# The first two batches of a packed-attention and two-layer MoE kernel, reordered by a list scheduler in single-engine steps

## The chip, the cores and the metric

The kernel runs on one core of one Trainium2 chip. The metric is the device time of one execution in microseconds (us), the median of several runs. The engines are TensorE (PE; its weight loads are PEld), VectorE (DVE), ScalarE (ACT), GpSimd (POOL) and SyncE (SP), which issues every DMA here.

## The reference

Eight batches, eight heads, 576 tokens, head dimension 64, 32 packed rows for each head, all in fp32. Attention runs twice: the packed rows `p` attend to `k`, `v`, and their result serves `q` as both keys and values. Two dense layers follow.

```python
def sm_attn(qq, kk, vv):
    s = scale * np.matmul(qq, kk.transpose(0, 1, 3, 2))
    s = s - np.max(s, axis=-1, keepdims=True)
    a = np.exp(s)
    a = a / (np.sum(a, axis=-1, keepdims=True) + 1e-09)
    return np.matmul(a, vv)
p_packed = sm_attn(p, k, v)
out = sm_attn(q, p_packed, p_packed)
x = out.transpose(0, 2, 1, 3).reshape(4608, 512)
h = np.maximum(np.maximum(x @ w1, x @ w2), x @ w3)   # w1..w3: 512 x 768
x = h @ w_out                                        # 768 x 512
h = x @ w_in                                         # 512 x 2048
return (h * np.cos(h)) @ moe2_w_out                  # 2048 x 512
```

## The kernel before, in words

A number that needs more than TensorE's fp32r format is kept as two halves, high (rounded) and low (the rest), and a product is three matmuls over the halves (`passes`). `split` makes them: a copy on ACT, a subtraction on DVE or POOL.

**Units.** A batch has two units (groups of four heads). Phase 1 of a unit makes its packed values: `ld_k`, `ld_v` (loads), `S1` (scores, 8 native fp32 matmuls), `S1m` (maximum), `E1` (exponential), `v` (halves of the values), `T1` (transposes), `PV1` (packed values), `BT` (their transpose, in two layouts `bt` and `wt`). Phase 2 makes the attention of the queries: `ld_q`, `S2` (scores), `S2t`, `S2r` (transpose to 32-wide blocks, maximum, subtraction), `X2a` (exponential), `X2b` (sum, reciprocal, multiplication), `X2t` (transpose back), `X2c` (halves). Batch 0 uses `Unit32`, whose `PV1` multiplies the raw values in native fp32 and needs no `v`; the others use `Unit`.

**Folds.** The packed values are multiplied into w1, w2, w3 once for two batches: `fold(b, j, g, pi)` is a quarter of a column group `j` (five groups: four of 512 columns, one of 256). Its three matmuls write the PSUM tile `zps`, ACT and DVE split it into `zx`, of which there are two buffers in the first two batches, and SP sends one half of it to the tile `z` of the even batch and the other to DRAM (`zd`), where the odd batch fetches it (`load_z`). `fold_first(g)` makes a whole half of group 0 for batch 0 alone, in six matmuls straight into `z`.

**Dense layers.** `gemm1(b, u, m)`, u from 0 to 17, multiplies `z` by the attention (12 matmuls of 288 columns) and every third result ends a maximum over three. `gemm2` is the second product (36 such matmuls for each of four d). The last layers run after all batches, with tiles of 512 tokens.

**Weight pieces.** w1, w2, w3 and w_out arrive as 24 pieces of 512 KB, as 64-bit floats, and are rebuilt on the chip: `sign` (POOL), `wc` (ACT), two bit operations on DVE (`wc`, `wm`), a rounding copy (ACT) and `low` (POOL). `conv_wa` does one piece and also finishes the one before. Pieces 8 and on land in the pool `wop`, which is opened when both units of batch 0 are done.

**Order.** Each engine executes its instructions in program order. Before, this order is written by hand: `START` lists the steps ahead of the batches, `FIRST`, `PLAN`, `PLAN0` and `FOLDS` put steps at positions u of the batches, and each position of batch 0 also converts a piece. A step such as `T1` issues its instructions on PE, ACT and DVE at once.

Of the kernel before, what the change touches and what calls it, by code (L numbers as in the profile page):

```python
# [19 lines left out]
MAGIC = 12582912.0  # L20


@with_exitstack
def tile_pack_attention_max_moe_cos_moe(
# [98 lines left out]
    with tc.manual_schedule():  # L123
# [4 lines left out]
        class Res:  # L128
            def __init__(self):
                ap = self.ap = actx.enter_context(tc.tile_pool(name="ap", bufs=1, side="right"))  # L130
                self.ps = actx.enter_context(tc.tile_pool(name="ps_a", bufs=1, space=PSUM, side="right"))
                self.pz = ap.tile([P, 2, P], F32, name="pz")
                self.bt = [[ap.tile([P, 2, P], F32, name=f"bt{o}{g}") for g in range(NG)] for o in range(2)]
                self.wt = [wtp.tile([P, 8, D], F32R, tag="x", name="wt") for _ in range(NWT)]
                self.mask = ap.tile([P, P], F32, name="mask")
                self.vhl = ap.tile([P, 2, NCH, 2 * P], F32R, name="vhl")

            def clear(self):
                nc.gpsimd.memset(self.pz, 0.0)
# [10 lines left out]
        class Res32:  # L150
            def __init__(self, n, ps):
# [4 lines left out]
                if n == 0:  # L156
                    self.pz1 = self.ap.tile([P, 2, P], F32, name="pz1")
                    nc.vector.memset(self.pz1, 0.0)
# [32 lines left out]
        class Unit:  # L191
            def lo(self, name):
                return nc.gpsimd if name == "v" else nc.vector

            def __init__(self, b, g):
                self.b, self.g = b, g
                self.res = res32[g] if b == 0 else res
                self.pz = res32[g].pz if b == 0 else res32[0].pz1 if (b, g) == (1, 1) else res.pz
                self.bt = res.bt[b % 2][g]
                self.wt = res.wt[b // 2 % 2 * NG + g]  # L200
# [40 lines left out]

            def v(self):
                self.vhl = self.res.vhl
                for c, n, rows, r in self.vr:
                    src = r[:rows, :n * 2 * P].rearrange("p (a e) -> p a e", a=n)
                    split(self.vhl[:rows, 0, c:c + n, :], self.vhl[:rows, 1, c:c + n, :], src, self.lo("v"))
# [26 lines left out]
            def E1(self):  # L273
                self.e = self.etile()
                nc.gpsimd.memset(self.e[:, S:], 0.0)
                nc.scalar.activation(
# [13 lines left out]

            def T1(self):
                src = self.tr()[:, :SP_].rearrange("p (c b d) -> p c b d", b=2, d=D)
                self.at = self.res.ap.tile([P, 2 * SP_], F32R, tag="at", name="at")
                av = self.at.rearrange("p (c b d) -> p c b d", b=4, d=D)
                split(av[:, :, ::3, :], av[:, :, 1:3, :], src)

            def PV1(self):
                ps = self.big()
# [9 lines left out]
                pv = self.res.ap.tile([P, P], F32, tag="pv", name="pv")  # L308
                for pi in range(2):
                    own, oth = slice(pi * D, pi * D + D), slice(D - pi * D, P - pi * D)  # L310
                    nc.scalar.copy(pv[own], ps[oth, pi, :P])
                    for j in (1, 0):
                        nc.vector.tensor_tensor(  # L313
                            out=pv[own], in0=pv[own], in1=ps[own, pi, j * P:(j + 1) * P], op=ALU.add
                        )
                self.recip()
                self.bd = self.res.ap.tile([P, P], F32, tag="bd", name="bd")
                nc.vector.scalar_tensor_tensor(
                    out=self.bd, in0=pv, scalar=self.st[:, 3:4], in1=self.res.mask, op0=ALU.mult, op1=ALU.mult
                )  # L320
# [37 lines left out]
            def X2b(self):  # L358
                t = self.t
                tb = t[:, :S].rearrange("p (a b) -> p a b", b=32)  # L360
                sm = self.ms[:, 1, :]
                nc.vector.tensor_reduce(out=sm, in_=tb, op=ALU.add, axis=AX.X)
                nc.vector.tensor_scalar(out=sm, in0=sm, scalar1=EPS, scalar2=None, op0=ALU.add)
                nc.vector.reciprocal(out=sm, in_=sm)
                self.lo("mul").tensor_tensor(
                    out=tb, in0=tb, in1=sm[:, :, None].to_broadcast([P, NB, 32]), op=ALU.mult
                )

# [3 lines left out]

            def X2c(self):
                h = at[self.b, self.g] = hp.tile([P, 2, S], F32R, tag="h", name="at")
                split(h[:, 0, :], h[:, 1, :], self.a[:, :S], self.lo("X"))

        class Unit32(Unit):
            def T1(self):
                ps = self.tr()
                self.at = self.res.ap.tile([P, SP_], F32, tag="at", name="at")  # L380
                h = 3 * P
                nc.scalar.copy(self.at[:, :h], ps[:, :h])
                nc.vector.tensor_copy(self.at[:, h:], ps[:, h:SP_])

            def PV1(self):
                ps = self.big()[:, 0, :]
# [11 lines left out]
                self.recip()  # L398
                self.bd = self.res.ap.tile([P, P], F32, tag="bd", name="bd")
                for pi in range(2):  # L400
                    own = slice(pi * D, pi * D + D)
                    nc.vector.scalar_tensor_tensor(
                        out=self.bd[own], in0=ps[own, pi * P:(pi + 1) * P], scalar=self.st[own, 3:4],
# [11 lines left out]
        def fold(b, j, g, pi):  # L415
# [11 lines left out]
            nx[0] += b > 0  # L427
            x = (wop if nx[0] % 3 == 2 else zx).tile([P, 2, UB * P], F32R, tag="w", name="zx")[:, :, :nw]
            split(x[:, 0, :], x[:, 1, :], ps)
            if pi == 0 and (b, j) != (0, 0):  # L430
                zt[b, j, g] = zp.tile([P, 2, UB * P], F32R, tag="w", name="z")
            zo = zd[b + 1, j, g]
            own, oth = slice(pi * D, pi * D + D), slice(D - pi * D, P - pi * D)
            if (b, j) != (0, 0):
                z = zt[b, j, g][:, :, :nw]
                nc.sync.dma_start(out=z[own].bitcast(F32), in_=x[own].bitcast(F32))
            nc.sync.dma_start(out=zo[oth], in_=x[oth].bitcast(F32))

        def fold_first(g):
            wt = units[0][g].wt  # L440
            ps = fps[0].tile([P, 512], F32, tag="f", name="zps")
            n = 0
            for pi in range(2):
                for x, y in passes:
# [3 lines left out]
                        w_mov(0, 2 * g + pi, y),  # L448
# [4 lines left out]
            z = zt[0, 0, g] = zp.tile([P, 2, UB * P], F32R, tag="w", name="z")  # L453
            split(z[:, 0, :], z[:, 1, :], ps)

        def load_z(b, j):
            nw = min(UB, NU - j * UB) * P
            for g in range(NG):
                zt[b, j, g] = zp.tile([P, 2, UB * P], F32R, tag="w", name="z")
                nc.sync.dma_start(out=zt[b, j, g][:, :, :nw].bitcast(F32), in_=zd[b, j, g])  # L460

        def gemm1(b, u, m):
            j, c = u // UB, (u % UB) * P
            ps = ps_m.tile([P, 2, 512], F32, tag="big", name="h")
            for hf in range(2):
                n = 0
                for g in range(NG):
                    for x, y in passes:
# [7 lines left out]
                        n += 1  # L476
            if u % 3 == 0:
# [4 lines left out]
        def gemm2(b, d, hf, hh):  # L482
            if hf == 0:
                g2ps[0] = ps_m.tile([P, 2, 512], F32, tag="big", name="x2")
            ps = g2ps[0]
            n = 0
            for f in range(NF):
                w = wa[NU + f]
                for x, y in passes:
# [7 lines left out]
                    n += 1  # L497
            if hf:
                s = mp.tile([P, S], F32, tag="m", name="x2s")
                nc.vector.tensor_copy(halves(s), ps[:, :, :HS])  # L500
                o = 0
                while o < S:
                    t, r = divmod(b * S + o, TT)
                    k = min(S - o, TT - r)
                    nc.sync.dma_start(out=x2d[t][:, d, r:r + k], in_=s[:, o:o + k])
                    o += k

        g2ps = [None]
# [22 lines left out]
        PLAN = {  # L531
# [5 lines left out]
        }  # L537
        PLAN0 = {
# [343 lines left out]
```

## Time and profile before

| | |
|---|---|
| median of 3 runs | 1458.03 us (1452.14 to 1458.88) |
| the profiled execution | 1458.1 us, span of its instructions 1456.2 us |
| busy, share of the span | PE 95%, PEld 81%, DVE 58%, ACT 37%, POOL 19% |
| granted TensorE clock, mean | 0.973 of full speed |

The page also cuts the span into 40 equal slices, of 36.4 us each. There the digits of PE are 7, 5, 6, 6, 8 and then 9 nearly throughout, and the granted clock is 9, 6, 7, 7 and then 9: what is not filled lies in the first five slices. Times below count from the start of the span.

### The profile page before, as it was taken

To read this page: it belongs to the slowest core of one execution; us is meant where nothing else is said; L and a number is where in the kernel's file an instruction comes from. 1 tells how busy PE (TensorE), PEld (TensorE's weight loads), DVE (VectorE), ACT (ScalarE), POOL (GpSimd) and SP (SyncE) were. 2 spreads that over 40 slices of the span, in tenths; PEclk is the share of its full clock that TensorE was granted. 3 is DMA by queue.
4 is the path that set the end of the run, shared out by engine and by line. 5 is a ranking of instruction groups with operands and counts; after the bars stand their busy time and mean duration, and the time that the engine had idled before them with its cause. 6 is when DMAs were issued, how large, how long until landed. Compare 5 with 4: busy or idle time off the path is not lost.

```text
span 1456.2 us, 18953 instructions
## 1 busy us (share of the span) xinstructions
PE 1378.1 (95%) x7110; PEld 1180.3 (81%) x7110; DVE 847.7 (58%) x1423; ACT 535.4 (37%) x962; POOL 270.3 (19%) x229
## 2 busy tenths in 40 slices
PE   7566899999999999899999999999999999999998
PEld 4455899999989999788678888888888888888887
DVE  5655645555555556568875555555555555556554
ACT  3444232523342333444443333333333333333333
POOL 3765330303121213764500000000000000000000
PEclk9677999999999999899999999999999999999999
DMA  8285355843765478543210010100101010010000
GB/s 298 104 236 168 121 180 163 229 142 122 217 177 186 126 194 277 193 147 100 82 59 1 0 58 1 58 0 12 47 1 58 1 54 5 0 58 1 30 1 29
DMA packets 72860, 143.33 MB, mean 98 GB/s; under 512 B 13632, under 2 KB 35136, under 8 KB 72768
## 3 DMA queue, kind: packets, MB, share of 16 engines
q1 hardware_dynamic: 72768, 142.12, 31.6%
q8 instruction: 56, 0.92, 0.3%
q14 instruction: 36, 0.29, 0.1%
HBM read 86.51 MB, written 37.75 MB: 85 GB/s over the span
## 4 chain that ended last, share of the span: by engine, by line
PE 78%; DVE 12%; issue 3%; ACT 3%; DMA 2%; POOL 1%; SPq 0%; DVEq 0%; ACTq 0%; POOLq 0%
PE po L810 24%; PE g L709 24%; PE h L469 11%; PE x L490 9%; PE big L252 4%; PE zps L420 3%; PE big L301 1%; DMA zd<-zx 1%; DVE wm L110 1%; DVE m L480 1%; DVE wc L110 1%; DVE pv L313 1%; DVE wm L113 1%; DVE y L721 1%; DVE y L730 1%
## 5 line engine op out<-in xcount | busy, mean ns | idle before, releaser
L810 PE MATMUL po<-w,gh 128*128 128x512 f32 x1728 | 425.1, 395 | 3.9 <-ACT gh L74 3.3
L709 PE MATMUL g<-x,w 128*128 128x512 f32 x1728 | 419.1, 391 | 0.8 <-DVE x2s L500 0.8
L810 PEld LDWEIGHTS po<-w,gh 128*128 128x128 f32 x1728 | 324.0, 188 | 82.2 <-ACT gh L74 5.9
L709 PEld LDWEIGHTS g<-x,w 128*128 128x128 f32 x1728 | 324.3, 188 | 72.6 <-DVE x2s L500 1.1
L469 PE MATMUL h<-at,z 128*128 128x288 f32 x1728 | 263.6, 309 | 10.7 <-DVE x2s L500 3.7
L469 PEld LDWEIGHTS h<-at,z 128*128 128x128 f32 x1728 | 247.7, 197 | 19.1 <-DVE m L480 7.2
L725 ACT ACTIVATE y<-y 128x512 f32<-128x512 f32 x144 | 91.0, 632 | 245.2 <-DVE y L722 245.2
L490 PE MATMUL x<-hh,w 128*128 128x288 f32 x1152 | 163.4, 299 | 3.1 <-DVE hh L75 1.9
L490 PEld LDWEIGHTS x<-hh,w 128*128 128x128 f32 x1152 | 157.6, 190 | 8.1 <-DVE hh L75 3.6
L75 DVE TENSOR_TENSOR gh<-y,gh 128x512 fp32r<-128x512 f32 x144 | 99.8, 693 | 98.9 <-ACT gh L74 98.9
L730 DVE TENSOR_TENSOR y<-y,g 128x512 f32<-128x512 f32 x144 | 98.9, 687 | 92.7 <-ACT y L725 92.7
L74 ACT CAST gh<-y 128x512 fp32r<-128x512 f32 x144 | 89.4, 621 | 125.4 <-DVE y L730 124.3
L718 ACT ACTIVATE y<-g 128x512 f32<-128x512 f32 x144 | 86.2, 599 | 130.7 <-PE g L709 130.7
L720 DVE TENSOR_SCALAR y<-y 128x512 f32<-128x512 f32 x144 | 61.4, 426 | 115.8 <-ACT y L718 115.8
L721 DVE TENSOR_TENSOR y<-y 128x512 f32<-128x512 f32 x144 | 100.9, 701 | 6.1 <-DVE y L720 0.5
L480 DVE TENSOR_TENSOR m<-m,h 128x576 f32<-128x576 f32 x96 | 72.3, 753 | 43.6 <-PE h L469 32.2
L92 POOL TENSOR_SCALAR w<-wraw 128x512 fp32r<-128x512 f32 x56 | 90.8, 1623 | 17.7 <-DMA wraw<-w 12.0
L85 POOL TENSOR_TENSOR w<-wm,w 128x512 fp32r<-128x512 f32 x56 | 73.4, 1311 | 104.2 <-ACT w L106 78.7
L420 PE MATMUL zps<-w,wt 128*128 128x512 f32 (+1 forms) x240 | 67.0, 396 | 27.0 <-DVE zx L75 27.0
L75 DVE TENSOR_TENSOR zx<-zps,zx 128x512 fp32r<-128x512 f32 (+1 forms) x80 | 50.6, 635 | 71.9 <-ACT zx L74 63.3
L75 POOL TENSOR_TENSOR hh<-m,hh 128x576 fp32r<-128x576 f32 x40 | 56.9, 1423 | 169.0 <-ACT hh L74 168.8
L74 ACT CAST zx<-zps 128x512 fp32r<-128x512 f32 (+1 forms) x80 | 43.1, 541 | 94.0 <-PE zps L420 34.5
(87 smaller groups left out, 950.6 us busy)
## 6 DMA issues: line engine op xcount, KB each, us to landing
zd<-zx SPq DMA_DIRECT2D x64, 256.0 KB, 3.6
z<-zd SPq DMA_DIRECT2D x32, 512.0 KB, 4.5
z<-zx SPq DMA_DIRECT2D x60, 256.0 KB, 3.2
wraw<-w_out SPq DMA_DIRECT2D x22, 512.0 KB, 4.0
raw<-kT SPq DMA_DIRECT2D x32, 288.0 KB, 4.3
wraw<-w SPq DMA_DIRECT2D x18, 512.0 KB, 6.1
raw<-qT SPq DMA_DIRECT2D x32, 288.0 KB, 4.5
xr<-x2d SPq DMA_DIRECT2D x36, 256.0 KB, 5.1
```

What stands on the lines that cost most here:

```text
L74: nc.scalar.copy(hi, src)
L75: eng.tensor_tensor(out=lo, in0=src, in1=hi.bitcast(F32), op=ALU.subtract)
L92: nc.gpsimd.tensor_scalar(out=w[:, 1, :], in0=hi32.bitcast(F32), scalar1=0.0, scalar2=None, op0=ALU.mult)
L420: nc.tensor.matmul(ps, wt[:, pi * 4 + x * 2:pi * 4 + x * 2 + 2, :].rearrange("p a b -> p (a b)"), w_mov(j, 2 * g + pi, y), start=(n == 0), ...
L469: nc.tensor.matmul(ps[:, hf, :HS], zt[b, j, g][:, x, c:c + P], at[b, g][:, y, hf * HS:(hf + 1) * HS], start=(n == 0), stop=(n == 3 * NG - 1),)
L480: nc.vector.tensor_tensor(out=halves(m), in0=halves(m), in1=ps[:, :, :HS], op=ALU.max)
L490: nc.tensor.matmul(ps[:, hf, :HS], w[:, x, d * P:(d + 1) * P], hh[f][:, y, hf * HS:(hf + 1) * HS], start=(n == 0), stop=(n == 3 * NF - 1),)
L709: nc.tensor.matmul(ps, w[:, a, kc * P:(kc + 1) * P], x2[t, kc][:, b, :], start=(n == 0), stop=(n == 3 * KC - 1),)
L721: nc.vector.tensor_tensor(out=y, in0=y, in1=r, op=ALU.subtract)
L725: nc.scalar.activation(out=r, in_=y, func=AF.Sin, scale=TWO_PI)
L730: nc.vector.tensor_tensor(out=r, in0=r, in1=ps, op=ALU.mult)
L810: nc.tensor.matmul(po[t][s], g[:, a, s * P:(s + 1) * P], w[:, b, :], start=(f == 0 and i == 0), stop=(f == NF2 - 1 and i == 2),)
```

## The change

The steps are cut so that each issues on one engine (`T1` becomes `Tp`, `Ta`, `Td`; `fold` becomes `fold_p`, `fold_a`, `fold_d`, `fold_z`; a piece becomes `sg`, `wt`, `ws`, `wm`, `wh`, `wl`). For batches 0 and 1 and what belongs to batches 2 and 3 in that time, a class `Order` keeps a table of the steps with their assumed durations, needs and buffers, and issues them in the order in which it expects them to start; of those ready at nearly the same time it takes the one with the longest rest. `low` and the low half of `hh` go to POOL or DVE, and the copies out of `gemm2` to ACT or DVE, whichever is expected to end first. From batch 2 on the hand-written positions stay.

Batch 1 now also uses `Unit32`. Column groups 0 and 1 (`alone`) get folds of batch 0's own, `full_p`, `full_a`, `full_d`, in the manner of `fold_first`; their four quarters then serve batch 1 alone. The raw loads and the piece loads run as two sequences that the scheduler interleaves.

```diff
+class Order:
+    LAT, LAND, RATE, NEAR, BIAS = 0.2, 1.8, 0.34, 0.3, 0.4
...
+            for name, c in best.items():
+                near = min(x[0] for x in c) + self.NEAR
+                x = min((x for x in c if x[0] <= near), key=lambda x: (x[1], x[0]))
+                if pick is None or x[0] < pick[1][0]:
+                    pick = name, x
...
-        units = {b: [(Unit if b else Unit32)(b, g) for g in range(NG)] for b in range(B)}
+        units = {b: [(Unit if b > 1 else Unit32)(b, g) for g in range(NG)] for b in range(B)}
...
+        alone = (0, 1)
...
+            only = b == 0 and j in alone
...
+            if not only:
                 z = zt[b, j, g][:, :, :nw]
                 nc.sync.dma_start(out=z[own].bitcast(F32), in_=x[own].bitcast(F32))
...
-        def fold_first(g):
+        def full_p(j, g):
             wt = units[0][g].wt
-            ps = fps[0].tile([P, 512], F32, tag="f", name="zps")
+            nw = min(UB, NU - j * UB) * P
+            ps = fx[j, g] = fps[0].tile([P, 512], F32, tag="f", name="zps")[:, :nw]
...
+        LOADS = "k0 k1 v0 v1 q0 q1 k2 k3 v2 v3 q2 q3 k4 v4 k5 v5 k6 v6 q4 k7 v7 q5 k8 v8".split()
...
+            add(
+                ("W", n), "SP", 0.6, lambda n=n: load_wa(n), ["wop"] * (n >= 8),
+                [(pool, ("W", n))], data=0.52,
+            )
...
+            add(
+                ("wl", n), (GE, VE), (1.28, 0.7), lambda eng, n=n: low(wa[n], wm[n], EITHER[eng]), [("wh", n)], [],
+                [("wm", n)],
+            )
...
+                add(
+                    last, "PE", 1.6, lambda b=b, u=u: gemm1_p(b, u), after, [("mm", ("h", b, u))],
+                    [("Z", b, j, g) for g in range(NG)] + [("att", 2 * b + g) for g in range(NG)],
+                )
...
+        order.run()
...
-        for b in range(B):
+        for b in range(2, B):
```

What this does to the order is seen best at three places.

PE, around the first `gemm1`. Before (`zps<-w,wt` from L445 is `fold_first`, `raw,pz` is `S1`, `ident,e` the transposes, `vhl,at` `PV1`, `ident,bd` `BT`, and `h<-at,z` from L469 `gemm1`):

```order
L445 MATMUL zps<-w,wt 128x512 x6
L252 MATMUL big<-raw_199,pz_160 128x288 x4
L288 MATMUL big<-ident,e 128x128 x5
L301 MATMUL big<-vhl,at 128x256 x10
L288 MATMUL big<-ident,e 128x128 x5
L469 MATMUL h<-at,z 128x288 x12
L329 MATMUL big<-ident,bd 128x128
L301 MATMUL big<-vhl,at 128x256 x10
```

Now (L648 is `full_p`, L573 the fp32 `PV1` of batch 1, L685 `gemm1`):

```order
L648 MATMUL zps<-w,wt 128x512 x6
L407 MATMUL big<-ident,e 128x128 x5
L685 MATMUL h<-at,z 128x288 x12
L367 MATMUL big<-raw_199,pz_139 128x288 x4
L685 MATMUL h<-at,z 128x288 x24
L573 MATMUL big<-raw_200,at 128x256 x4
L573 MATMUL big<-raw_201,at 128x256
L648 MATMUL zps<-w,wt 128x512 x6
```

Three steps of `gemm1` now stand ahead of batch 1's `PV1`, and unit 3's scores stand behind the first of them.

DVE, in phase 2 of batch 0's units (`e` holds the scores, `ms` the block maxima and sums; `wc`, `wm` are a piece). Before:

```order
L344 STREAM_TRANSPOSE e<-big 128x576
L349 TENSOR_REDUCE ms<-e 128x18
L350 TENSOR_TENSOR e<-e,ms 128x576
L110 SCALAR_TENSOR_TENSOR wc<-wc,w 128x512
L113 SCALAR_TENSOR_TENSOR wm<-wraw,wc 128x512
L344 STREAM_TRANSPOSE e<-big 128x576
L362 TENSOR_REDUCE ms<-e 128x18
L363 TENSOR_SCALAR ms<-ms 128x18
L364 RECIPROCAL ms<-ms 128x18
L365 TENSOR_TENSOR e<-e,ms 128x576
```

Now:

```order
L501 STREAM_TRANSPOSE e<-big 128x576
L508 TENSOR_REDUCE ms<-e 128x18
L512 TENSOR_TENSOR e<-e,ms 128x576
L501 STREAM_TRANSPOSE e<-big 128x576
L508 TENSOR_REDUCE ms<-e 128x18
L512 TENSOR_TENSOR e<-e,ms 128x576
L525 TENSOR_REDUCE ms<-e 128x18
L529 TENSOR_SCALAR ms<-ms 128x18
L530 RECIPROCAL ms<-ms 128x18
```

The pieces that stood between the two units' rows now stand ahead of them (four pieces) or behind (from the fifth).

PE, in batch 0's `gemm1`. Before (L420 is a quarter, one in nearly each position):

```order
L420 MATMUL zps<-w,wt 128x512 x6
L469 MATMUL h<-at,z 128x288 x12
L420 MATMUL zps<-w,wt 128x512 x6
L469 MATMUL h<-at,z 128x288 x12
L420 MATMUL zps<-w,wt 128x512 x3
L252 MATMUL big<-raw,pz 128x288 x4
```

Now (L474 and L367 are unit 3's `Bp` and unit 2's `S2`, L606 a quarter):

```order
L474 MATMUL big<-ident,bd 128x128
L367 MATMUL big<-raw,bt_142 128x288 x4
L606 MATMUL zps<-w,wt 128x512 x3
L685 MATMUL h<-at,z 128x288 x12
L606 MATMUL zps<-w,wt 128x512 x3
```

The first quarter of all now stands behind four steps of `gemm1`, and 12 quarters (groups 2, 3, 4) stand ahead of the 16th; the eight of groups 0 and 1 stand behind that, most of them inside `gemm2`.

## Rows read from the trace of the kernel before

**Rows 1.** Busy time of each engine by stage (start:end, length, engines, clock, DMA).

```profile
core 0: us, PE busy (x) PEld busy (x) DVE busy (x) ACT busy (x) POOL busy (x), PEclk, DMA share, GB/s
0.00:57.50 57.50, 36.90 (x122) 25.38 (x123) 36.18 (x68) 22.43 (x46) 32.04 (x43) 0.81 0.73 254
57.50:161.30 103.80, 70.78 (x346) 61.08 (x344) 58.55 (x104) 45.24 (x91) 60.11 (x48) 0.81 0.55 155
161.30:184.60 23.30, 22.91 (x153) 22.30 (x154) 10.16 (x16) 2.36 (x5) 0.15 (x1) 0.93 0.50 170
184.60:252.50 67.90, 67.01 (x454) 62.86 (x453) 36.53 (x65) 21.27 (x43) 13.70 (x13) 1.00 0.53 160
252.50:1456.20 1203.70, 1180.51 (x6041) 1008.72 (x6039) 706.31 (x1172) 444.12 (x777) 164.26 (x125) 0.99 0.26 81
```

**Rows 2.** Timeline of PE (start us, us, instruction, idle before and releaser).

```profile
12.72 2.62 PE L391 MATMUL big<-raw,at 128*128 128x256 f32 x10 [1.03 <-DVE st L324]
...
57.54 2.94 PE L469 MATMUL h<-at,z 128*128 128x288 f32 x12
...
68.90 0.95 PE L420 MATMUL zps<-w,wt 128*128 128x512 f32 x3
...
150.62 0.62 PE L420 MATMUL zps<-w,wt 128*128 128x256 f32 x3 [1.63 <-DVE zx L75]
...
161.95 4.18 PE L490 MATMUL x<-hh,w 128*128 128x288 f32 x18 [0.40 <-DVE m L480]
...
252.56 1.97 PE L469 MATMUL h<-at,z 128*128 128x288 f32 x12
```

**Rows 3.** Waits from 57.5 to 161.3 us (total, times, longest).

```profile
PE zps L420 <- DVE zx L75: 27.0, 12, 4.6
```

**Rows 4.** Chain that ended last, one quarter and the landing behind another.

```profile
72.67 0.59 ACT zx L74
...
73.29 0.70 DVE zx L75
...
74.53 3.33 DMA zd<-zx
...
88.15 6.38 DMA zd<-zx
```

**Rows 5.** Timeline of DVE, phase 2 of batch 0's units, first and last row.

```profile
22.94 0.78 DVE L344 STREAM_TRANSPOSE e<-big 128x576 f32<-128x576 f32 x1 [0.85 <-PE big L252]
...
44.27 1.77 DVE L75 TENSOR_TENSOR at<-e,at 128x576 fp32r<-128x576 f32 x1 [1.35 <-ACT at L74]
```

**Rows 6.** Windows to 252.5 us, tile `e` alone (columns as in the first group).

```profile
0.00:252.50 252.50, 7.41 (x40) 5.40 (x40) 34.08 (x42) 14.82 (x28) 1.28 (x9) 0.87 0.58 180
```

**Rows 7.** DVE groups to 252.5 us: busy, mean ns of one.

```profile
L363 DVE TENSOR_SCALAR ms<-ms 128x18 f32<-128x18 f32 x6 | 3.0, 492 | 0.2
...
L364 DVE RECIPROCAL ms<-ms 128x18 f32<-128x18 f32 x6 | 1.6, 267 | 0.2
```

**Rows 8.** DVE groups from 57.5 to 161.3 us.

```profile
L110 DVE SCALAR_TENSOR_TENSOR wc<-wc,w 128x512 uint32<-128x512 uint32 x16 | 11.1, 696 | 17.5 <-ACT wc L103 14.1 <-POOL w L92 2.1 <-POOL vhl L75 1.3
L75 DVE TENSOR_TENSOR zx<-zps,zx 128x512 fp32r<-128x512 f32 x16 | 11.0, 687 | 14.9 <-ACT zx L74 14.9
L113 DVE SCALAR_TENSOR_TENSOR wm<-wraw,wc 128x512 uint32<-128x512 uint32 x16 | 11.0, 687 | 0.5
L480 DVE TENSOR_TENSOR m<-m,h 128x576 f32<-128x576 f32 x11 | 8.3, 751 | 2.0 <-PE h L469 1.9
```

**Rows 9.** Chain that ended last, from 224 to 276 us, at full clock.

```profile
228.18 0.69 PE zps L420 x3
228.87 1.94 PE big L252 x8
230.81 2.40 PE x L490 x18
...
252.94 1.59 PE h L469 x12
```

More of the change, by code (lines that the diff above doesn't have):

```diff
@@ L138, in clear @@
             def clear(self):
-                nc.gpsimd.memset(self.pz, 0.0)
+                for pz in self.pz:
+                    nc.gpsimd.memset(pz, 0.0)
                 for w in self.wt[:NG]:
@@ L596, in att_pos @@
                     fold(bb, j, *QUARTERS[r])
-            for _, who, ahead, what in (steps if b else steps0).get(p, []):
+            for _, who, ahead, what in steps.get(p, []):
                 us = units.get(b + ahead)
@@ new lines, in tile_pack_attention_max_moe_cos_moe @@
+        VE, GE = "DVE", "POOL"
+        EITHER = {"DVE": nc.vector, "POOL": nc.gpsimd}
+        LOADS = "k0 k1 v0 v1 q0 q1 k2 k3 v2 v3 q2 q3 k4 v4 k5 v5 k6 v6 q4 k7 v7 q5 k8 v8".split()
+        slots = [("raw", ("r", n)) for n in range(NRAW)]
+        slots += [("hp", ("r", NRAW + n // 2)) for n in range(2 * (NF + 3))]
+        prev, raws = None, {}
+        for n, item in enumerate(LOADS):
+            kind, i = item[0], int(item[1])
+            need = 3 if kind == "v" else 2
+            use, take = [], []
+            for k in range(need):
+                if slots:
+                    pool, token = slots.pop(0)
+                    order.owner[token] = pool
+                    use.append(token)
+                else:
+                    take.append(("raw", ("raw", item, k)))
+                    use.append(("raw", item, k))
+            raws[item] = use
+            after = []
+            if kind == "k" and i >= 4:
+                after.append(("S1", i - 2))
+            fn = {"k": uu[i].ld_k, "v": uu[i].ld_v, "q": uu[i].ld_q}[kind]
+            add(item, "SP", 0.55 * (4 if kind == "k" else need), fn, after, take, use, data=0.6)
+            order.ops[item].queued = [prev] if prev else []
+            prev = item
@@ new lines, in tile_pack_attention_max_moe_cos_moe, with piece, quarter @@
+        order.hold([("w", n) for n in range(NU + NF)])
+        def piece(j, kc):
+            return j * KC + (kc if j < NJ - 1 else kc // 2)
+        def quarter(b, j, g, pi, pool):
+            key, args = ("F", b, j, g, pi), (b, j, g, pi)
+            w = 1.0 if j < NJ - 1 else 0.55
+            only = b == 0 and j in alone
+            add(
+                key + ("p",), "PE", 0.7 * w, lambda: fold_p(*args),
+                [("Bd", 2 * b + g), ("Bd", 2 * b + 2 + g), ("wl", piece(j, 2 * g + pi))] + ["ps_f"] * (b > 0),
+                [(pool, key + ("f",))],
+            )
+            add(key + ("a",), "ACT", 0.6 * w, lambda: fold_a(*args), [key + ("p",)],
+                [("wop" if b and (j * UB + 2 * g + pi) % 3 == 1 else "zx", key + ("x",))], [key + ("f",)])
+            add(key + ("d",), VE, 0.69 * w, lambda: fold_d(*args), [key + ("a",)], [], [key + ("f",), key + ("x",)])
+            add(
+                key + ("z",), "SP", 1.1, lambda: fold_z(*args), [key + ("d",)] + [("F", b, j, g, 0, "z")] * pi,
+                [("zp", ("Z", b, j, g))] * (pi == 0 and not only), [key + ("x",)] + [("Z", b, j, g)] * (not only), data=0.26,
+            )
@@ new lines, in swap_f @@
+        def swap_f():
+            cctx.close()
+            fps[0] = mctx.enter_context(tc.tile_pool(name="ps_f", bufs=2, space=PSUM, reuse_waits="tile"))
+        add(
+            "ps_f", "none", 0.0, swap_f,
+            [("wm", n) for n in range(NU + NF)]
+            + [("F", 0, j, g, pi, "d") for j in range(NJ) for g in range(NG) for pi in range(2)],
+        )
+        for j, rs in ((0, range(UB)), (1, (0, 1))):
+            for r in rs:
+                g, pi = QUARTERS[r]
+                quarter(2, j, g, pi, "f2")
+                order.ops["F", 2, j, g, pi, "p"].after.append(("H", 1, NU - 1) if j == 0 else ("X", 1, 1, 1))
+                order.ops["F", 2, j, g, pi, "z"].bonus = 16.0
```

636 lines of the change are left out of this document (469 added, 167 removed), and 8 rows, old and new, of tables (PLAN, PLAN0).

## The prediction

> **What bounds the kernel now.** I read the stages first, then the chain, then the waits inside the stage that the chain shows to be loose. The windows by stage [rows 1] cut the run at four marks on PE's timeline [rows 2]: the first `gemm1` matmul at 57.5 us, the first `gemm2` at 162.0, and the first `gemm1` of batch 2 at 252.6; batch 1 begins at 184.6. From 184.6 on PE is busy 67.0 of 67.9 us and then 1180.5 of 1203.7, at a clock of 0.99 to 1.00: nothing is to be had there except by less PE work. Up to 161.3 it is busy 36.9 of 57.5 and 70.8 of 103.8 us, and the clock is 0.81 in both. So the loss lies ahead of 161.3, as idle time and as a low clock.
>
> What PE would need for the 103.8 us stage at full clock follows from the chain in a stage that runs dense [rows 9]: 1.59 us for one `gemm1` step, 0.69 for a quarter, 1.94 for a unit's scores. 18 steps make 28.6 and 20 quarters (four of them of half width) some 12.4; with the attention of units 2 to 4 it comes to about 51, against 103.8. The largest wait of PE there is for DVE to free the only `zps` buffer, 27.0 us in 12 waits [rows 3]. DVE itself is busy 58.6 of 103.8 us, so it isn't full but late: the chain [rows 4] shows a quarter as ACT 0.59, DVE 0.70, the issue and 3.33 us of landing, and since there are two `zx` buffers the next but one waits for that landing; at another place the landing took 6.38. Between the first and the last of the 20 quarters lie 81.7 us [rows 2], 4.3 for each. The stage is a fixed sequence of short dependent pieces in which no engine is full, and that is what another order can change.
>
> **The change part by part.** I go through the four stages; behind the last of them every engine's sequence is the same as before, so its 1203.7 us stand.
>
> *To the first `gemm1`.* Phase 2 of batch 0's units ran on DVE from 22.94 to 46.04 us [rows 5]. Its own rows are 34.08 us on tile `e` for six units [rows 6], 5.68 for one, and 0.492 + 0.267 for the small reciprocal rows [rows 7]: 6.44 us a unit, 12.9 for two. The other 10 us were pieces, a maximum and the split of `z`. Now the two units' rows stand together. Ahead of them the change puts four pieces of two bit operations, 1.38 us each [rows 8], where DVE waits for batch 0's packed values, and sends the piece loads ahead of some raw loads. I let that cost 0.5 us: phase 2 starts at 23.4 and with 1 us of gaps ends at 37.3. Behind it DVE has unit 2's maximum (0.9), two splits of `z` (0.69 each) and a piece (1.4): 41.0 us is when `z` and the attention are both there. PE's order allows it, since only scores and transposes of unit 2 stand ahead. Before, everything was there by 46 as well, and PE's order put batch 1's `PV1` with its halves in front until 57.5. Mark 1: 41, against 57.5.
>
> *Batch 0's `gemm1`.* DVE's rows between are 20 pieces at 1.38 (27.7), 10 low halves that now run on DVE, at the price of the like row of a quarter, 0.687 (6.9), nine quarters and three `z` at 0.687 (8.2), four half quarters at 0.42 (1.7), 12 maxima at 0.751 (9.0), unit 2's phase 2 without its end (5.7), two `hh` (1.5) and some 5 us of small rows: 65.7 us in all [rows 6 to 8]. That is the floor for the stage. The first quarter stands behind 22 us of these; at 0.9 of DVE's time it comes at 66. Then 12 quarters in two buffers: held 0.59 + 0.70 + 0.5 + 3.33 and some gaps, 5.2 us, a buffer gives one quarter in 2.6 us; with a landing of 6.38 it is 4.1 [rows 4]. Data come denser now (the same weights in three quarters of the time), so I take 3.6, nearer the upper end: 43 us, to 109. Three more steps of `gemm1` and the end of the last `hh` add 7.5. Mark 2: 117, and DVE is then busy 65.7 of 76. Bounds: 107 if DVE is the only limit, 123 at 4.1 us a quarter.
>
> PE fits below: 28.6 for the steps, 6.9 for the 12 quarters, 1.4 for two more, 2.8 for the own folds of group 1, 7.8 for four scores, 5.2 for batch 1's two fp32 `PV1` at 2.62 [rows 2, 9], 52.7 us at full clock. Before, about 51 us of such work showed as 70.8 busy [rows 1], 1.4 times as much; by that ratio it is 73 of 76 us. This is close, and the cover that would be gone first.
>
> *The own folds and the fp32 values.* Group 1's own folds are 12 matmuls, 2.8 us of PE, and two more splits, 1.4 us each on ACT and DVE; they take four quarters (2.8 us of PE, which stay for batch 1) out of the time in which `gemm1` waits for them. Batch 1's values lose the POOL and ACT halves and pay a little PE for it; no step of batch 0's stage is released by POOL then. I price both inside the sums above and give them nothing else.
>
> *`gemm2` of batch 0.* 8 x 2.40, six quarters at 0.69, one scores of 1.94, one `PV1` (1.2 at most half of its 2.62 row): 26.5 us, and 1.5 for a clock that isn't full throughout. Eight quarters at 2.6 to 3.6 us are 21 to 29, of which the first two lie ahead: they fit. Batch 1's `z` comes from DRAM; its fourth quarter lies some 10 us into the stage, and two landings of 3.3 to 6.4 behind it end before 28. Mark 3: 145, where 184.6 was; the stage takes 28 for 23.3 because four quarters and one unit's scores moved into it.
>
> *Batch 1.* 18 x 1.59, 8 x 2.40, seven quarters, six scores for five before, and one or two `PV1` and transposes more: about 5 us over the 67.9 of before. Mark 4: 145 + 73 = 218, where 252.5 was.
>
> The sum: 252.5 - 218 = 34.5 us, so 1458.1 - 34.5 = 1423.6, rounded to **1424 us**. The profiled execution (1458.1) and the median (1458.03) agree, so the difference is taken from either.
>
> **What the skill says of two of these terms.** The Trainium skill, DMA: Bandwidth & Descriptors, Anatomy of one DMA, gives about 2.0 us fixed and the bytes over 436 GB/s for a transfer that GpSimd issues. By it, an estimate, 256 KB would land in 2.6 us. The two rows here say 3.33 and 6.38 [rows 4], issued by SP and beside other transfers; I go by them. By the page the quarters would not limit the stage, which is the second case below.
>
> **The rivals.**
>
> *DVE alone sets the stage.* Landings stay short and DVE's queue has no holes: mark 2 is 107, the rest as above, and the time 1414. For it: DVE was never over 0.65 busy in these stages on average [rows 1], so its order was loose. Against: ACT's answers lie between DVE's rows of a piece and of a quarter, and cost DVE 14.1 and 14.9 us of idle time before [rows 8].
>
> *TensorE stays at a low clock.* The granted clock was 0.81 in the first two stages with PE busy two thirds of the time [rows 1]. If the idle gaps remain, 52.7 us of work at 1.2 GHz is 105 us: mark 2 is 146 at worst, the time 1453; half way, 1438. For it: a quarter's wait lies between all steps, as before. Against: PE has the same work in 76 us, so it is busier, and at 184.6 it went to 1.00 as soon as it was dense. The Trainium skill, TensorE: Matmul & The Clock Gate, Part 1, says that the throttled state is the default and activity lifts it; the rows agree in that the clock is full just where PE is dense.
>
> *The change only moves the wait.* The quarters keep their 4.3 us [rows 2] and batch 0's stage stays bound by them and by the pieces, as long as before: mark 2 is 41 + 104 = 145 and the time about 1452, which is no change worth the name.
>
> *Slower: landings behind the pieces.* With weights, raw loads and quarters nearer together, each landing of a quarter could grow. 20 quarters in two buffers lose half of each added us, 10 us for one. The gain of 34.5 is gone when a landing takes 3.5 us more than the 5.3 that my 3.6 us contains (7.2 for a buffer, less 1.9 for what isn't landing), so from 8.8 us on, and at 10.3 the time is 1474. For it: SP is one queue, and a load that waits for a free buffer holds the quarters behind it. Against: 6.38 is the longest that the chain shows, and the DMA share of 0.55 [rows 1] leaves room.
>
> **How the numbers follow.** My forecast, within some 10 us of 1424: 0.62. DVE alone, 1414 or less: 0.12. Low clock, 1434 to 1450: 0.14. Wait only moved, about 1452: 0.07. Slower: 0.05. The forecast's own spread carries mark 2 from 107 to 123 and 3 us in each of the two stages behind. For 8 in 10 the range reaches into the clock's rival and nearly to DVE's floor with dense later stages: 1408 to 1444. A measurement of this kernel tells 0.5% (7 us) from no change. Faster by more than that, under 1450.7, holds the first three cases, nearly all of a fourth's better half and some of what is left: 0.9; the same 0.05; slower 0.05.
>
> **What would show it.** Right: the first `gemm1` near 41 us and the first `gemm2` near 117; DVE above 0.8 busy between; quarters 3 to 4 us apart and the wait of `zps` for DVE below 15 us; the first `gemm1` of batch 2 near 218, and 1203 to 1205 us from there to the end. Wrong: `gemm1` starting after 50 (then piece loads delayed the raw data, or pieces held DVE ahead of phase 2); quarters over 4.3 us apart with landings over 6 (the slower rival); PE over 0.9 busy at a clock under 0.75 (the clock); a tail that isn't 1204 us, since I took its order to be the same.

## The result, and the profile after

The changed kernel takes 1419.57 us (median of 4 runs, 1413.4 to 1421.36), the one before 1455.09 in the runs beside it; the ratio is 0.9749, 95% interval 0.9705 to 0.9794. The profiled execution has a span of 1419.2 us.

The windows by stage, cut at the same marks (first `gemm1`, first `gemm2`, batch 1, batch 2), with the columns of [rows 1]:

```profile
core 0: us, PE busy (x) PEld busy (x) DVE busy (x) ACT busy (x) POOL busy (x), PEclk, DMA share, GB/s
0.00:40.50 40.50, 27.52 (x100) 20.17 (x100) 25.02 (x53) 14.46 (x29) 22.17 (x35) 0.92 0.96 324
40.50:118.30 77.80, 63.40 (x336) 54.21 (x335) 63.15 (x105) 44.01 (x83) 47.74 (x35) 0.89 0.64 184
118.30:143.40 25.10, 25.10 (x174) 24.20 (x173) 9.53 (x15) 7.55 (x13) 0.00 (x0) 0.98 0.55 157
143.40:214.50 71.10, 70.60 (x479) 66.11 (x478) 43.87 (x82) 29.17 (x61) 12.11 (x14) 1.00 0.60 187
214.50:1419.20 1204.70, 1179.34 (x6041) 1006.48 (x6039) 705.47 (x1172) 444.21 (x777) 164.25 (x125) 1.00 0.26 81
```

Against [rows 1] the marks have moved from 57.5, 161.3, 184.6 and 252.5 us to 40.5, 118.3, 143.4 and 214.5. Of the 38.0 us, 17.0 are won before the first `gemm1`, another 26.0 in batch 0's `gemm1`, and 1.8 and 3.2 are given back in the next two stages; the rest is 1.0 us longer. In the second stage DVE is now busy 63.15 of 77.8 us (0.81, before 0.56), PE 0.81 (0.68), and the clock is 0.89 (0.81). GpSimd is idle in `gemm2`.

PE's timeline at the marks and at the first and last of the 12 quarters (groups 2, 3 and 4) that batch 0's `gemm1` needs:

```profile
40.48 2.06 PE L685 MATMUL h<-at,z 128*128 128x288 f32 x12
...
64.18 1.39 PE L606 MATMUL zps<-w,wt 128*128 128x512 f32 x3
...
104.75 0.51 PE L606 MATMUL zps<-w,wt 128*128 128x256 f32 x3
...
118.31 8.07 PE L714 MATMUL x<-hh,w 128*128 128x288 f32 x54
...
214.57 1.97 PE L685 MATMUL h<-at,z 128*128 128x288 f32 x12
```

The quarters stand 40.57 / 11 = 3.7 us apart, before 4.3 [rows 2]. The waits of the second stage (total, times, longest):

```profile
ACT zx L618 <- DMA zd<-zx: 8.7, 4, 3.6
...
PE zps L606 <- DVE zx L623: 5.9, 3, 4.3
```

PE's wait for DVE is down from 27.0 us [rows 3] to 5.9, and ACT waits 8.7 us in four waits for the landing of an older quarter. The chain runs through that as well:

```profile
72.51 0.48 SPq L634
...
73.03 5.99 DMA zd<-zx
...
79.12 0.59 ACT zx L618
...
79.74 0.70 DVE zx L623
...
80.49 1.65 PE zps L606 x3
```

Read alone, this says what the prediction said: a quarter lands in 3.3 [rows 4] to 6 us and the next but one waits. The experiments bear this out for a part of the stage only.

### The profile page after: what moved, and what is told of

Read it like the earlier page. It is cut to its first block, busy times and chain, and to the rows that moved or that the text cites. A ratio compares the mean times of both kernels' runs of the same rounds, so it can differ in the third digit from the quotient of the medians.

```text
span 1419.2 us, 18953 instructions
## 1 busy us (share of the span) xinstructions
PE 1366.0 (96%) x7122; PEld 1171.2 (83%) x7122; DVE 847.0 (60%) x1425; ACT 539.4 (38%) x962; POOL 246.3 (17%) x209
## 4 chain that ended last, share of the span: by engine, by line
PE 77%; DVE 8%; DMA 3%; ACT 2%; issue 2%; POOL 1%; SPq 1%; DVEq 0%; ACTq 0%; POOLq 0%
PE po L1255 25%; PE g L1163 25%; PE h L685 11%; PE x L714 9%; PE big L367 4%; PE zps L606 3%; DVE wm L219 1%; DMA zd<-zx 1%; PE big L432 1%; DVE y L1175 1%; DVE m L700 1%; DVE y L1184 1%; DMA z<-zd 1%; ACT gh L183 1%; DMA xr<-x2d 1%
## 5 line engine op out<-in xcount | busy, mean ns | idle before, releaser
L685 PE MATMUL h<-at,z 128*128 128x288 f32 x1728 | 257.9, 304 | 16.0 <-DMA z<-zx 3.9
L685 PEld LDWEIGHTS h<-at,z 128*128 128x128 f32 x1728 | 242.0, 193 | 24.7 <-DVE m L700 6.8
L1174 DVE TENSOR_SCALAR y<-y 128x512 f32<-128x512 f32 x144 | 61.3, 426 | 116.1 <-ACT y L1172 116.1
L194 POOL TENSOR_TENSOR w<-wm,w 128x512 fp32r<-128x512 f32 x46 | 60.8, 1322 | 84.0 <-ACT w L215 64.6
L606 PE MATMUL zps<-w,wt 128*128 128x512 f32 (+1 forms) x240 | 64.6, 385 | 6.4 <-DVE zx L623 5.9
L1176 DVE TENSOR_SCALAR y<-y 128x512 f32<-128x512 f32 x144 | 66.4, 461 | 4.9
```

Source lines behind the costliest of these rows:

```text
L606: nc.tensor.matmul(ps, wt[:, pi * 4 + x * 2:pi * 4 + x * 2 + 2, :].rearrange("p a b -> p (a b)"), w_mov(j, 2 * g + pi, y), start=(n == 0), ...
L685: nc.tensor.matmul(ps[:, hf, :HS], zt[b, j, g][:, x, c:c + P], at[b, g][:, y, hf * HS:(hf + 1) * HS], start=(n == 0), stop=(n == 3 * NG - 1),)
```

## The experiments

All edits are to the changed kernel, if nothing else is said, and the scheduler then makes a new order for the two batches; so no run changes one thing alone. Theory A is the prediction's term for the quarters (the two `zx` buffers and the landings space them), taken for the whole length of batch 0's `gemm1`, though the prediction too counted DVE's rows ahead of the first quarter; theory B puts the gain down to the own folds and the fp32 values, theory C says that DVE's work makes that length. Each was timed in five rounds beside the kernel before; the marks come from one profile each, and how far a mark wanders from one execution of a kernel to the next wasn't measured.

| run | median us | ratio to before, 95% | first gemm1 | first gemm2 | batch 1 | batch 2 |
|---|---|---|---|---|---|---|
| changed kernel | 1419.57 | 0.9705 to 0.9794 | 40.5 | 118.3 | 143.4 | 214.6 |
| own folds for group 0 alone | 1417.43 | 0.9715 to 0.9760 | 40.2 | 126.9 | 149.1 | 218.6 |
| fp32r values in batch 1 | 1415.72 | 0.9706 to 0.9751 | 42.0 | 113.8 | 140.9 | 212.1 |
| third buffer | 1422.68 | 0.9750 to 0.9795 | 40.8 | 122.8 | 146.8 | 217.2 |
| lows on GpSimd | 1411.62 | 0.9672 to 0.9718 | 40.8 | 110.4 | 135.0 | 206.1 |
| lows on VectorE | 1424.19 | 0.9771 to 0.9814 | 41.3 | 112.0 | 148.3 | 218.8 |
| third buffer, lows on GpSimd | 1412.00 | 0.9693 to 0.9726 | 40.1 | 112.7 | 136.8 | 207.2 |
| fp32r values, lows on GpSimd | 1414.13 | 0.9704 to 0.9734 | 41.4 | 115.8 | 138.3 | 209.5 |
| the same, `hh` on GpSimd | 1416.10 | 0.9714 to 0.9746 | 40.6 | 115.8 | 138.3 | 210.0 |
| assumed landing 2.6 us | 1418.41 | 0.9727 to 0.9776 | 40.0 | 115.5 | 140.5 | 217.1 |
| before, early `gemm1` by hand | 1466.43 | 1.0056 to 1.0102 | 41.3 | 176.4 | 199.5 | 265.7 |
| before, fp32 values | 1452.82 | 0.9976 to 1.0001 | 58.0 | 161.3 | 184.4 | 250.6 |
| before, own folds | 1448.34 | 0.9931 to 0.9975 | 58.0 | 153.1 | 177.3 | 243.5 |

What lies behind the last mark is the same sequence throughout and took 1200 to 1205 us in these profiles, so times that differ by less than 5 us are compared by the marks.

**Own folds for group 0 alone.**

```diff
-        alone = (0, 1)
+        alone = (0,)
```

> The changed kernel with own folds for column group 0 alone, so that 16 quarters and not 12 stand ahead of the end of batch 0's gemm1. Theory A (the spacing of the quarters, set by the two zx buffers and their landings, makes the length of that stage): four more quarters at 3.7 us lengthen it by up to 15 us, and gemm2's stage gives some 3 back: 1428 to 1432 us, the first gemm2 near 130 us. Theory B (the gain of the change is the own folds and the fp32 values, the order only arranges them): 20 us and more, over 1438. Theory C (VectorE is the limit): two splits less, 1417 to 1420.

The time is no longer, so B falls for this part; A's 1428 to 1432 is missed too, and the time is C's. The marks say more: with 16 quarters ahead the first `gemm2` comes 8.6 us later, over half of A's price, but `gemm2` of batch 0 is 2.9 us shorter and batch 1 comes 5.7 later, batch 2 4.0. The first and the last of the 16:

```profile
60.56 1.65 PE L606 MATMUL zps<-w,wt 128*128 128x512 f32 x3
...
115.58 0.62 PE L606 MATMUL zps<-w,wt 128*128 128x256 f32 x3 [0.25 <-DVE zx L623]
```

They stand 55.02 / 15 = 3.7 us apart, as the 12 did. So between the quarters A's price is there, some 14 us for four more; a part of it is saved again ahead of the first quarter, which comes 3.6 us earlier, and behind the last one.

**Batch 1's values in fp32r halves.** The units of batch 1 are `Unit` again, and their table entries follow.

```diff
-        units = {b: [(Unit if b > 1 else Unit32)(b, g) for g in range(NG)] for b in range(B)}
+        units = {b: [(Unit if b > 0 else Unit32)(b, g) for g in range(NG)] for b in range(B)}
```

> The changed kernel with batch 1's packed values from fp32r halves again (Unit in place of Unit32), so GpSimd and ScalarE make six halves for each of its two units. Theory A: TensorE saves 3 us, the first quarter comes 3 to 5 us later behind GpSimd's halves: 1421 to 1426. Theory B: 10 us or more, over 1430. Theory C: a little more VectorE work (two sums for each half and wider copies, some 4 us): 1423.

All three expected a loss, and there is none: the median is 3.9 us lower, batch 2's mark 2.5 earlier. So the fp32 values show no gain here.

**A third buffer.** The scheduler's table has the same edit.

```diff
-            x = (wop if b and (j * UB + 2 * g + pi) % 3 == 1 else zx).tile([P, 2, UB * P], F32R, tag="w", name="zx")[:, :, :ps.shape[-1]]
+            x = (wop if (j * UB + 2 * g + pi) % 3 == 1 else zx).tile([P, 2, UB * P], F32R, tag="w", name="zx")[:, :, :ps.shape[-1]]
```

> The changed kernel with every third quarter of the first two batches in a buffer of the pool wop, as it already is for the later batches, so that three quarters can be under way. Theory A: quarters 2.6 to 3 us apart in place of 3.7, the first gemm2 near 110 us, 1412 to 1416 in all. Theory C: VectorE is the limit and nothing changes, 1418 to 1421. A rival to both: the buffer is taken from the weight pieces, which then come later, 1422 or more.

1422.68: not faster. The windows show what else happened:

```profile
40.80:122.80 82.00, 68.08 (x355) 56.73 (x353) 70.64 (x118) 45.90 (x89) 45.60 (x34) 0.90 0.65 193
```

DVE carries 70.64 us in that stage in place of 63.15, since the scheduler put 13 more rows there, most of them unit 3's phase 2. GpSimd waited 15.2 us for quarters to leave `wop`:

```profile
POOL w L201 <- DMA zd<-zx: 15.2, 3, 7.0
```

So this run alone doesn't tell the buffer from the rows; a later one comes nearer.

**Low halves on GpSimd alone.**

```diff
-                ("wl", n), (GE, VE), (1.28, 0.7), lambda eng, n=n: low(wa[n], wm[n], EITHER[eng]), [("wh", n)], [],
+                ("wl", n), GE, 1.28, lambda n=n: low(wa[n], wm[n], nc.gpsimd), [("wh", n)], [],
```

> The changed kernel with every low half of a weight piece on GpSimd (10 of the 24 were on VectorE in that stage). Theory A: VectorE has 8 us less in the stage, but isn't the limit; GpSimd's queue gets 13 us longer and some folds wait for their pieces: 1419 to 1424. Theory C: the stage shrinks by 6 to 8 us, 1411 to 1413.

1411.62, as C expected and A did not. The windows of the two stages:

```profile
40.80:110.40 69.60, 59.77 (x337) 51.47 (x335) 56.21 (x95) 43.59 (x83) 57.67 (x44) 0.95 0.70 210
110.40:135.00 24.60, 24.60 (x175) 23.78 (x174) 10.30 (x17) 7.62 (x13) 0.00 (x0) 1.00 0.58 162
```

DVE has 6.9 us less and the stage is 8.2 us shorter; DVE's share is 0.81 again (56.21 of 69.6; 63.15 of 77.8). The wait for landings is still there, 6.9 us in three:

```profile
ACT zx L618 <- DMA zd<-zx: 6.9, 3, 4.4
```

PE's timeline, first and twelfth quarter:

```profile
59.96 0.97 PE L606 MATMUL zps<-w,wt 128*128 128x512 f32 x3
...
100.11 0.52 PE L606 MATMUL zps<-w,wt 128*128 128x256 f32 x3
```

They keep their 3.7 us; where the 8 us lie is told further below. It is the fastest kernel here, 8 us below the changed one by the medians; the two intervals against the kernel before overlap a little (0.9705 to 0.9718), the marks show the same 8 us (110.4 for 118.3 at the first `gemm2`, 206.1 for 214.6 at batch 2), and the run with the third buffer as well, further below, has nearly the same median.

**Low halves on VectorE alone.** The same line with `VE, 0.7` and `nc.vector`.

> The changed kernel with every low half of a weight piece on VectorE: 24 in place of 10, some 10 more of them in batch 0's gemm1. Theory C (VectorE's work, at about 0.81 of its time, makes the length of that stage): 10 x 0.69 / 0.81 = 8 to 9 us longer, the first gemm2 near 127 us, 1424 to 1430. Theory A (the spacing of the quarters by buffers and landings): no more than 2 us, since neither the buffers nor the transfers change, and GpSimd is relieved: 1417 to 1421.

The time is C's, the place is not. The first `gemm2` comes at 112.0 and not near 127, earlier than in the changed kernel, and DVE has nearly the same work in that stage, 62.43 us, at a share of 0.88:

```profile
41.30:112.00 70.70, 56.87 (x324) 47.93 (x323) 62.43 (x102) 39.56 (x75) 30.78 (x22) 0.98 0.62 183
```

So the mean share of 0.81 is no constant of the stage. It is batch 1 that comes late, 148.3. The chain there:

```profile
135.41 1.95 PE big L367 x8
137.38 0.80 DVE e L501
...
139.78 0.69 ACT e L522
140.50 0.76 DVE ms L525
...
142.59 0.79 DVE e L545
```

The scheduler put most of unit 2's phase 2 from `gemm1` into `gemm2`, and unit 3's from the start of `gemm2` (118.96 us in the changed kernel) to behind its last matmuls, where nothing covers it. DVE's work up to batch 1 is 26.6 + 62.4 + 19.1 = 108.1 us, in the changed kernel 25.0 + 63.2 + 9.5 = 97.7, with the lows on GpSimd 25.0 + 56.2 + 10.3 = 91.5; batch 1 begins at 148.3, 143.4 and 135.0. More work of DVE goes with a later batch 1, but that is a tendency and no law: with fp32r values it is 100.3 and batch 1 begins at 140.9, and with 97 to 98 us four runs begin it at 136.8 to 143.4.

**The third buffer without the extra rows.** Both edits above, the third buffer and the lows on GpSimd.

> The run with the low halves on GpSimd, and the third buffer for the quarters as well, so that the scheduler can no longer put more low halves on VectorE beside it. Theory C: the buffer changes nothing, 1409 to 1414, as without it. Theory A: the quarters draw nearer and the first gemm2 comes 4 us or more earlier than at 110 us, 1404 to 1407.

1412.00, as without the buffer. The stage, with its waits:

```profile
40.10:112.70 72.60, 63.08 (x354) 54.46 (x353) 64.35 (x109) 45.04 (x87) 56.74 (x44) 0.93 0.70 212
```

```profile
ACT zx L618 <- DMA zd<-zx: 1.1, 2, 0.7
```

The wait for landings is nearly gone, 1.1 us in place of 6.9, and neither does the stage end earlier nor do the quarters draw nearer:

```profile
59.02 0.96 PE L606 MATMUL zps<-w,wt 128*128 128x512 f32 x3
...
101.27 0.52 PE L606 MATMUL zps<-w,wt 128*128 128x256 f32 x3
```

They are 3.8 us apart, which A did not expect. But it isn't a clean comparison. The scheduler moved unit 3's phase 2 into `gemm1` and DVE has 64.35 us there in place of 56.21, at a share of 0.89 (64.35 of 72.6) in place of 0.81; GpSimd waits 6.2 us for quarters to leave `wop`, and the chain runs through GpSimd's rows. So the buffer may well have taken idle time off DVE, and the added rows filled it. What a third buffer is worth with the order held fixed is open.

**The gains together.** The fp32r values with the lows on GpSimd, and then the `hh` lows on GpSimd as well.

> Low halves on GpSimd and batch 1's values from fp32r halves. The two gains of the single runs (8 us and up to 4) add up if each takes work off the engine that sets the stage: 1406 to 1409. They don't if GpSimd, which now has both the lows and the values' halves, becomes what the folds wait for: 1413 or more.

> As the run with fp32r values and low halves on GpSimd, and the low halves of hh in the first two batches on GpSimd too. Theory C: two or three rows of 0.75 to 1.06 us less on VectorE in the stage, 1 to 3 us: 1404 to 1408. Against it: the last hh of a batch is what gemm2 waits for, and GpSimd takes 1.4 us for it in place of 0.75, so batch 1's end loses 1 us and the whole is the same.

1414.13 and 1416.10: they don't add up, and the marks of batches 1 and 2 fall 3 to 4 us behind those of the lows alone. That GpSimd's longer queue is the reason was expected but isn't shown: PE's wait for `zps` is 9.4 us in the first and 5.2 in the second, 7.0 with the lows alone.

**A longer assumed landing.** `LAND` 2.6 in place of 1.8.

> The changed kernel with the scheduler's assumed landing of a DMA at 2.6 us in place of 1.8, nearer to the 3.3 us of the traces; only the order changes. Theory A: the first quarters and loads are placed a little earlier against the rest, 1414 to 1420. Rival: the order is robust against this number, 1418 to 1421.

1418.41, the same. The gain doesn't hang on this number.

**Parts alone, in the kernel before.** First the early `gemm1` by hand:

```diff
-            0: "2:PV1 3:v 3:T1", 1: "2:BT 3:PV1", 2: "3:BT 1:0 1:1", 3: "1:2 1:3",
+            0: "2:E1 2:v", 1: "3:S1 3:S1m 3:E1 2:T1", 2: "2:PV1 3:v 3:T1", 3: "2:BT 3:PV1", 4: "3:BT 1:0 1:1 1:2 1:3",
...
-            "0:X2a 1:S2t 0:X2b c 1:S2r z:0 1:X2a 0:X2t c 2:S1 1:X2b 2:S1m 0:X2c c 1:X2t z:1 2:E1 2:v 1:X2c c 3:S1 3:S1m "
-            "3:E1 c 2:T1 n"
+            "0:X2a 1:S2t 0:X2b c 1:S2r z:0 1:X2a 0:X2t c 2:S1 1:X2b 2:S1m 0:X2c c 1:X2t z:1 1:X2c c c n"
```

> The kernel before, with one part of the new order by hand: batch 1's phase 1 starts behind the first steps of batch 0's gemm1, and group 1's quarters one position later. Theory A: the first gemm1 comes at 46 to 48 us in place of 57.5, but the quarters need batch 1's packed values, which come no earlier, so the first gemm2 moves by less than 4 us: 1451 to 1456 (before 1455). Rival: the 10 us are carried to the end, 1445.

It is slower, ratio 1.0079, which neither side expected. PE's timeline, first `gemm1`, first quarter, first `gemm2`:

```profile
41.27 0.92 PE L469 MATMUL h<-at,z 128*128 128x288 f32 x3
...
84.42 1.19 PE L420 MATMUL zps<-w,wt 128*128 128x512 f32 x3
...
176.35 2.89 PE L490 MATMUL x<-hh,w 128*128 128x288 f32 x18 [0.39 <-DVE m L480]
```

`gemm1` starts 16 us earlier and the first quarter 15.5 us later (68.90 in [rows 2]); the first `gemm2` comes 14.4 later. What counts is when batch 1's packed values are there, not when `gemm1` starts. From the first quarter to the first `gemm2` it is 91.9 us here and 93.1 before.

Then the other two parts, `Unit32` for batch 1 and own folds for group 1 (its quarters at positions 16 to 19):

> The kernel before with batch 1's values in native fp32, and nothing else. Theory A: batch 1's packed values come some 3 us earlier, since no GpSimd halves stand in front, and the rest waits as before: 1450 to 1453. Theory B: a third or more of the gain, under 1444.

> The kernel before with own folds for group 1 as well, its four quarters moved to positions 16 to 19, and nothing else. Theory A: four quarters at 4.3 us less ahead of batch 0's gemm1, of which the pieces, one in each position, take half back: 1445 to 1450. Theory B: 1440 or less. Rival: the positions are paced by the pieces and not by the quarters, 1453 to 1456.

The fp32 values bring 2 us by the medians, and the interval holds nothing as well (0.9976 to 1.0001). The own folds bring 6.5 (1448.34, inside A's 1445 to 1450): the stage from first quarter to first `gemm2` shrinks from 93.1 to 80.6 us; the first quarter comes 3.6 us later, and `gemm2` of batch 0 is longer by some 1.5.

## Why the prediction was right

**The marks.** 41, 117, 145 and 218 were forecast, 40.5, 118.3, 143.4 and 214.6 came. The two later stages were sized 3 and 2 us too long: into the first I had put 1.5 us for a clock loss that PE, dense there, did not have (0.98) and one unit's scores of 1.94 us that do not stand in it, and the second holds some 3 us more than before and not 5. The rest, forecast as unchanged at 1203.7, took 1204.7, so 34.5 us were forecast and 35.5 measured (medians 1455.09 and 1419.57).

**To the first `gemm1`: right in the time, partly by luck.** DVE's phase 2 began at 23.56 us, forecast 23.4, and ended at 35.3, two us before the 37.3 of the sum. What the sum left out is that the second own fold stands on PE between the two splits of `z`; it waits for the first split and ends at 39.8:

```profile
33.83 1.43 DVE L553 TENSOR_TENSOR at<-e,at 128x576 fp32r<-128x576 f32 x2
```

```profile
36.86 2.90 PE L648 MATMUL zps<-w,wt 128*128 128x512 f32 x6 [6.78 <-DVE z L665]
```

The two errors cancel. That this mark is worth its 17 us was taken for granted, and the run by hand shows that it isn't by itself: there the same early mark cost 11.6 us in the end.

**Batch 0's `gemm1`: three stretches, and two limits.** The sum had DVE's rows up to the first quarter, then 12 quarters at 3.6 us, then an end of 7.5 us. The windows, cut at the first and the twelfth quarter, in the changed kernel:

```profile
40.50:64.18 23.68, 20.84 (x105) 16.81 (x104) 21.87 (x39) 14.61 (x29) 19.39 (x14) 0.93 0.56 194
64.18:104.75 40.57, 31.95 (x176) 28.64 (x175) 28.87 (x47) 21.85 (x40) 19.55 (x16) 0.87 0.73 199
104.75:118.30 13.55, 10.60 (x60) 8.76 (x59) 12.41 (x21) 7.55 (x14) 8.80 (x7) 0.92 0.51 124
```

and with the lows on GpSimd:

```profile
40.80:59.96 19.16, 17.45 (x97) 14.44 (x95) 16.11 (x29) 12.85 (x25) 17.97 (x14) 0.98 0.60 212
59.96:100.11 40.15, 32.78 (x184) 28.91 (x183) 31.57 (x54) 24.43 (x47) 32.29 (x26) 0.91 0.81 237
100.11:110.40 10.29, 9.55 (x61) 8.12 (x59) 8.53 (x13) 6.31 (x11) 7.42 (x6) 1.00 0.42 99
```

In the changed kernel DVE is busy 0.92 of the first and of the last stretch and 0.71 of the one between; 0.81 is the mean of these. With the lows off DVE the first stretch has 5.8 us less of DVE's work and is 4.5 us shorter, the last has 3.9 less and is 3.3 shorter. The middle one has 2.7 us more of it and is 0.4 us shorter: there DVE's work does not make the length. Behind the twelfth quarter PE waits for DVE ahead of unit 3's scores, 2.52 us in the changed kernel and 0.53 with the lows on GpSimd:

```profile
115.39 3.53 PE L367 MATMUL big<-raw,bt 128*128 128x288 f32 x8 [2.52 <-DVE at L421]
```

```profile
108.58 2.18 PE L367 MATMUL big<-raw,bt 128*128 128x288 f32 x8 [0.53 <-DVE at L421]
```

Ahead of the first quarter PE is nearly as full as DVE (20.84 of 23.68 us) and has 3.4 us less to do with the lows on GpSimd as well, as the scheduler put fewer of its steps there; how much of the 4.5 us is DVE's alone isn't separated. The windows of the other runs of the changed kernel go the same way. Ahead of the first quarter DVE's work runs from 13.3 to 22.5 us, and the length with it from 17.0 to 24.3. Between the 12 quarters, six runs with two buffers have 28.9 to 34.5 us of DVE's work in 39.0 to 43.3 us, in no order; only three runs in which DVE has 36.6 to 38.4 us there, two of them with the third buffer, lie on the long side, at 42.3 to 46.2.

So the prediction's parts held where it put them: 22 us of rows at 0.9 ahead of the first quarter (21.87 at 0.92 measured), and quarters near 3.6 us apart (3.7). The end was sized too short: from the start of the twelfth quarter it is 13.55 us, where the sum has 3.6 + 7.5; the sum filled it with PE's steps, and DVE is busy 0.92 of it. The first quarter came 1.8 us before its 66. Errors of both signs cancel, so that mark 2 is met to 1.3 us is in part luck.

What sets the 3.7 us is argued and not shown. The chain and ACT's waits name the landings, 16 quarters keep the same spacing, and up to 34.5 us DVE's work doesn't move it; but the third buffer, with the lows on GpSimd, took the waits away and the spacing stayed, with DVE then busy 0.89 of that stretch (37.74 of 42.25 us). Either DVE's added rows took the landings' place as the limit, or the landings weren't it.

**The low halves on DVE.** I priced the ten at 6.9 us; they measured 8.1, and taking them off DVE brought 8.

**Own folds and fp32 values: priced inside the sums, and right to give them nothing else.** Each can be undone singly without loss, and each alone in the kernel before brings 6.5 us and next to nothing. So the order seems to carry the gain, or most of it; with both undone at once it wasn't tried, nor were the interleaved loads undone.

**The rivals.** The clock was 0.89 in the second stage with PE busy 0.81 of the time, against 0.81 at 0.68 before. PE's wait for the quarters fell to 5.9 us. Landings of quarters in that stage (least, median, longest):

```profile
DMA to landing us min/median/max: 2.4/3.3/7.2
```

The longest stays under the 8.8 us of the slow case. DVE alone, with mark 2 at 107, fits the outer two stretches and not the whole stage.

What stays open: whether landings or something else set the distance of the quarters, and what a third buffer brings by itself; the scheduler reorders with every edit, and a run with the order held fixed wasn't made.

## What to carry to other kernels

A stage's mean busy share can hide stretches with different limits: here 0.81 was 0.92, 0.71 and 0.92. Cut a stage where the steps change their kind before asking for its limit, take rows off the engine that looks full, and see which of the stretches gets shorter; a wait that the chain names speaks for its own stretch alone. Moving one step of a sequence forward is worth only what the next dependent step gains by it; here the date of the first fold decided, and the first matmul of the layer did not. A scheduler that may choose between two engines by who ends first can fill the engine that limits a stretch; fixing that choice by hand was worth another 8 us.

## What was not expected of the hardware

The low halves took longer on DVE than the rows from which I priced them. DVE groups of the changed kernel from 40.5 to 118.3 us:

```profile
L194 DVE TENSOR_TENSOR w<-wm,w 128x512 fp32r<-128x512 f32 x10 | 8.1, 806 | 0.1
L623 DVE TENSOR_TENSOR zx<-zps,zx 128x512 fp32r<-128x512 f32 x10 | 6.9, 686 | 6.9 <-ACT zx L618 6.9
L1054 DVE TENSOR_TENSOR hh<-m,hh 128x576 fp32r<-128x576 f32 x2 | 2.1, 1064 | 0.0
```

The first two groups subtract tiles of the same size; the one that reads PSUM (`zx`) takes 686 ns, and the other (`w`), with both inputs in SBUF, 806 on average; the two rows of `hh`, counted at 0.75 us each, took 1.06. DVE's and GpSimd's timelines at some of the rows of `w`:

```profile
46.26 0.68 DVE L194 TENSOR_TENSOR w<-wm,w 128x512 fp32r<-128x512 f32 x1
...
58.70 1.33 DVE L194 TENSOR_TENSOR w<-wm,w 128x512 fp32r<-128x512 f32 x1
...
85.72 0.69 DVE L194 TENSOR_TENSOR w<-wm,w 128x512 fp32r<-128x512 f32 x1
```

```profile
43.85 7.53 POOL L201 TENSOR_SCALAR w<-wraw 128x512 fp32r<-128x512 f32 x5
...
58.20 1.27 POOL L194 TENSOR_TENSOR w<-wm,w 128x512 fp32r<-128x512 f32 x1
...
83.93 1.28 POOL L194 TENSOR_TENSOR w<-wm,w 128x512 fp32r<-128x512 f32 x1 [1.23 <-ACT w L956]
```

With GpSimd idle, at 85.72 us, such a row takes 0.69 us, no longer than from PSUM. At 58.70 it falls into GpSimd's like subtraction, takes 1.33 us and ends 0.56 us behind it (60.03, 59.47). At 46.26 it runs amid GpSimd's five scalings and isn't held up. The Trainium skill, SBUF — State Buffer, section SBUF: two separate sides, says that a VectorE operation with two SBUF inputs and a GpSimd operation that reads SBUF take a shared port pair in turn, each for the whole instruction. The row at 58.70 agrees; the one at 46.26 does not, or GpSimd's times, which are rough, mislead there.
